# Loads for the norms asked for one norm earlier, and the wide tiles of x loaded once, in the sixth and ninth gate and up pass

## The chip, the cores and the metric

The kernel runs on one core of one Trainium2 chip. The metric is the device time of one execution, in microseconds (us).

## The reference, cut to what matters

`x` has 2048 rows of 512 numbers in fp32. Four layers follow each other, a Fourier mixing layer and a gated feed-forward layer, twice:

```python
x = x + A(layernorm(x))        # layer 0
x = x + B(layernorm(x))        # layer 1
x = x + A(layernorm(x))        # layer 2
x = x + B(layernorm(x))        # layer 3

def A(x):                      # real part of a DFT over the hidden and the row dimension
    a, b = x @ dft_hid_re.T, x @ dft_hid_im.T
    return dft_seq_re @ a - dft_seq_im @ b

def B(x):                      # w_gate, w_up: 512 x 1792, w_down: 1792 x 512
    return (gelu(x @ w_gate) * (x @ w_up)) @ w_down
```

## The kernel before, in words

**Products.** Every fp32 product is made of three matmuls (`mm3`, L208 to L210): both operands are split into a rounded part and a remainder (`split`: ScalarE copies the rounded part at L151, VectorE subtracts it at L153), and high by high, high by low and low by high are summed in PSUM. Blocks are multiplied by a scheme with seven products in place of eight (pieces named A11, A12, S1 to S4, A22), whose sums and differences are VectorE's (L184, L188, L191).

**Stages.** `mix(layer)` runs layers 0 and 2. `geglu(w, layer)` runs layers 1 and 3, each for two halves of the rows, w = 0 and w = 1 (1024 rows each). A half has 14 passes `up(n)` over the gate and up weights (7 products each), with the first products of the down projection between them (`beside(n)`: in an odd pass A11 of pair (n-1)//2, in an even one A12). Then comes the `late` list: the other down products, 36 of them when all seven pairs are done that way. `SEVEN` gives the pairs: seven in three halves (layer 1 w 0, layer 1 w 1, layer 3 w 0), where `pairs == NP`, and five in the last half (layer 3 w 1).

**The wide tiles.** The down projection's results are turned back by VectorE and added to `x` in a wide tile of 128 x 2048 fp32 (`turned_rows`), one for each 512 rows: part 0 in the buffer `xwide`, part 1 in the buffer `wide`. `load_turned(part)` (L1254) fills such a tile with four DMAs of 256 KB on SyncE's queue (L1258). `rows_done` (L1271) writes it out. In the kernel before, a half with seven pairs calls `load_turned(0)` twice: in pass 14 (`beside(13)`, L1230) and once more behind the passes (L1348). Nothing reads the first copy. `load_turned(1)` stands a third into the `late` list (L1385). The buffer `wide` is also that of the turned rows of the norms (L670), from which a DMA at L675 takes them to DRAM.

**The norms.** While w = 0 runs, the rows of w = 1 are normalized (`block_steps(layer, 1)`, `norm(i)`, eight of 128 rows), one every nine steps, a step being about a product. The first rows of w = 0 are normalized in the mix ahead of it. Each norm's rows come in four DMAs of 64 KB (`x_load_mixed`, L245). ScalarE then sums them (L564), sums the squares (L566), GpSimd makes the root (L567, L568), ScalarE scales (L590), VectorE turns (L672). L664 says which rows norm i asks for: norm 0 those of the norms 0, 1, 2, and norm i those of norm i + 2.

**Streams.** The weights of the down products come through a list of items on SyncE's queue (L327, tile `s<-wc`, one DMA each); `stream["last"]` is the newest of these DMAs. `too_far` (L331) holds such an item to two places ahead of its use in the passes and to six ahead in the `late` list (`NEAR`). The pieces of the gate and up weights are loaded at L1009 (`s<-wb`) two passes ahead; in layer 1 w 0 they are made from raw weights in place of that. In layer 1 w 1 the sums for the next layer's norms are made ahead (`terms_ahead`), with rows loaded one ahead at L236.

**Order.** `TileContext(nc, schedule_with_timeline_sim=True)` orders each engine's instructions by the times of a simulation at build time. So an instruction that nothing holds back may stand in its engine's queue far ahead of its place in the code; the queue itself runs in order. `tc.issue_after(ins)` puts what is made inside it behind `ins` on the same engine. SyncE issues most loads; GpSimd issues most stores.

**The other work of ScalarE in a pass.** It copies sums out of PSUM (L195, L202) and applies the gelu (L1019); PSUM banks come free by it, and TensorE goes on into them.

Of the kernel before, what the change touches and what calls it, by code (L numbers as in the profile page):

```python
# [21 lines left out]
NT = TB // P  # L22
# [15 lines left out]
FORE = {0: 4, 2: 4}  # L38
MADE = 5
LEAD = 3  # L40
NK = NS // 2
SEED_AT = 3
MIXED = 4
# [4 lines left out]
def fnet_geglu(ctx: ExitStack, tc: tile.TileContext, x_in, ws, wh, wgu, wdn, wdc, out):  # L48
# [32 lines left out]
    nc = tc.nc  # L81
# [235 lines left out]
    stream = {"loaded": 0, "split": 0, "used": 0, "more": 0}  # L317
# [129 lines left out]
    NP = NF // 2  # L447

    def down_order(layer, w):
# [6 lines left out]
        late = [("S1", k) for k in range(LEAD)]  # L456
        late += [p for k in range(n) for p in [("S2", k)] + [("S1", k + LEAD)] * (k + LEAD < n)]
        late.insert(LEAD + 2, up.pop())
# [195 lines left out]
    def block_steps(layer, w):  # L654

        zt, t, wide = {}, {}, {}
        turned = [dram.tile([P, NT * D], F32, name=f"t{layer}_{w}_{part}") for part in range(2)]

        def norm(i):

            def run():
                r0 = w * 2 * NT
                end = 2 * NT if w else i // NT * NT + NT
                for k in range(i if i == 0 or i + NT == end and not w else i + 2, min(i + 3, end)):  # L664
                    fresh["mixed", r0 + k] = x_load_mixed(layer, r0 + k)
                z = normed(layer, r0 + i, True)
                part, n = divmod(i, NT)
                if n == 0:
                    assert not sb.out("z")
                    wide[part] = tpool.tile([P, NT * D], F32, name="wide")  # L670
                to = wide[part].rearrange("p (b n t) -> p b n t", n=NT, t=32)
                nc.vector.transpose(to[:, :, n], z.rearrange("p (b t) -> p b t", t=32))  # L672
                sb.put(z)
                if n == NT - 1:
                    nc.gpsimd.dma_start(turned[part], wide.pop(part))  # L675
            return run

        def fetch(c):

            def run():  # L680
                for part in range(2):
                    v = zt[c, part] = sb.get()
                    for i in range(P // 32):
                        cols = turned[part][:, (c * 4 + i) * P:(c * 4 + i + 1) * P]
                        to = v[i * 32:(i + 1) * 32]
                        (nc.gpsimd if w == 0 else nc.sync).dma_start(
                            to.rearrange("p (j t) -> p j t", t=P), cols.rearrange("(j p) t -> p j t", p=32)
                        )
            return run

        def difference(a, b):
            v = sb.get()
            minus(v, a, b)
            return v

        def first(c):
            def run():
                v = t[f"B{1 + c // 2}1", c % 2] = zt.pop((c, 0))
                blocks[f"B{1 + c // 2}1", c % 2] = split_slot(v)
            return run  # L700

        def second(c):
            def run():
                v = zt.pop((c, 1))
                if c < 2:
                    t["B12", c] = v
                    t["T1", c] = difference(v, t["B11", c])
                    sb.put(t.pop(("B11", c)))
                else:
                    c0 = c - 2  # L710
                    t["T2", c0] = difference(v, t["T1", c0])
                    t["T3", c0] = difference(v, t["B12", c0])
                    sb.put(t.pop(("B12", c0)))
                    blocks["B22", c0] = split_slot(v)
                    sb.put(v)
            return run

        def fourth(c):
            def run():
                t["T4", c] = difference(t["B21", c], t["T2", c])  # L720
                sb.put(t.pop(("B21", c)))
            return run

        def divide(name, c):
            def run():
                blocks[name, c] = split_slot(t[name, c])
                sb.put(t.pop((name, c)))
            return run

        one = [norm(i) for i in range(2 * NT)]  # L730
        two = [fetch(c) for c in range(ND)] + [first(c) for c in range(ND)] + [second(c) for c in range(ND)]
        two += [fourth(c) for c in range(2)]
        two += [divide(name, c) for name in ("T2", "T3", "T1", "T4") for c in range(2)]
        return one, two
# [287 lines left out]
    def geglu(w, layer):  # L1022
# [69 lines left out]
        def up(n):  # L1092
            if n + 3 in making:
                making[n + 3][0]()
            if n + 2 in making:
                queue.extend(making[n + 2][1])
            if n > 2:
                for _ in range(DOWN_RUNS[3]):
                    if down_making:
                        down_making.pop(0)()  # L1100
            product(n, chain[n], "S2", "T2", False, True)
            u[n] = copied(chain[n])
            down = beside(n)
            next(down, None)
            side[n] = ps8.get()
            product(n, side[n], "S1", "T1", True, True)
            w4[n] = copied(side[n])
            next(down, None)
            first(n + 1)
            product(n, chain[n], "S3", "T3", False, True)  # L1110
            v = w4.pop(n)
            plus(v, v, chain[n])
            finished(n, 1, 1, v)
            sb.put(v)
            next(down, None)
            product(n, side[n], "S4", "B22", False, True)
            v = u.pop(n)
            plus(v, v, side[n])
            ps8.put(side.pop(n))
            finished(n, 0, 1, v)  # L1120
            sb.put(v)
            next(down, None)
            second(n + 1)
            if pairs == NP:
                for name, k in down_order(layer, w)[1][:max(0, n - EARLY_FROM) * EARLY_EACH]:
                    if k in h4:
                        prepared(name, k)
            product(n, chain[n], "A22", "T4", False, True)
            ps = chain.pop(n)
            if n % 2 == 0:  # L1130
                v = copied(ps)
                finished(n, 1, 0, v)
                sb.put(v)
            else:
                finished(n, 1, 0, ps)
            ps8.put(ps)
            for _ in down:
                pass
# [8 lines left out]
        pairs = SEVEN.get((layer, w), 0)  # L1147
# [73 lines left out]
        def beside(n):  # L1221

            if plain_down:
                return down_steps(n - LAG, 0) if n >= LAG else iter(())
            k = (n - 1) // 2
            if k >= pairs:
                return iter(())
            if n % 2:
                if k == pairs - 1:
                    load_turned(0)  # L1230
                bs["A11", k] = split_slot(h[2 * k, 0])
                return down_product("A11", k)
            if n:
                pair_combined(k)
                return down_product("A12", k)
            return iter(())
# [11 lines left out]
        def rows_moved(at, part, run):  # L1248

            for p in range(NT):  # L1250
                v = xturned[part][p * 32:(p + 1) * 32]
                run(v.rearrange("t (j e) -> t j e", e=P), turned_view(at, part)[p])

        def load_turned(part):  # L1254
            assert part or not sb.out("x")
            pool = tpool if part else upool
            xturned[part] = pool.tile([P, NT * D], F32, name="wide" if part else "xwide")
            rows_moved(layer, part, lambda v, outside: nc.sync.dma_start(v, outside))  # L1258

        def turned_rows(part, c, src):  # L1260

# [82 lines left out]
                slow.pop(0)()  # L1344
        if plain_down:
            load_rows(0)
        elif pairs == NP:
            load_turned(0)  # L1348
        if w == 0:
            queue.extend([None] * 4 + others[len(ahead_of_all):ND] + ([] if ahead_of_all else [None] * 4) + others[ND:])  # L1350
        elif before_mix:
# [19 lines left out]
        else:  # L1371
# [3 lines left out]
            for i, (name, k) in enumerate(late):  # L1375
                for more in late[i:i + EARLY + 1]:
                    prepared(*more)
                for _ in down_product(name, k):
                    pass
                if not before_mix or i % 3 == 0:  # L1380
                    step()
                if before_mix and i == len(late) // 2:
                    stream["more"] = MORE
                if i == len(late) // 3:
                    load_turned(1)  # L1385
                    if w == 0:
                        queue[:2 * len(ahead)] = [run for pair in zip(ahead, queue) for run in pair] + queue[len(ahead):2 * len(ahead)]
                while w == 0 and len(queue) > 2 * (len(late) - 1 - i):
                    step()
# [118 lines left out]
```

## Time and profile before

| | |
|---|---|
| median of 3 runs | 1611.77 us (1610.68 to 1614.64) |
| the profiled execution's own time | 1611.43 us |
| its span, first to last instruction | 1609.7 us |
| granted TensorE clock, mean | 0.998 of full speed |
| busy TensorE / VectorE / ScalarE / GpSimd | 99% / 70% / 55% / 17% |
| moved by DMA | 419.14 MB, mean 260 GB/s |

The span is shorter than the execution's own time by 1.7 us, which lie around the first and last instruction. A row of a group gives line, engine, operation, names as out<-in with buffer numbers left out, shapes and count. A row of the timeline gives the start and the length in us, the engine (SPq is SyncE's queue), the line, the count, and in brackets how long the engine was idle before it and what ended that. A row of the windows gives the busy time of each engine in a stretch, with the number of instructions, then the granted clock, the busy share of the DMA engines and the rate.

### The profile page before, as it was taken

To read this page: it belongs to the slowest core of one execution; us is meant where nothing else is said; L and a number is where in the kernel's file an instruction comes from. 1 tells how busy PE (TensorE), PEld (TensorE's weight loads), DVE (VectorE), ACT (ScalarE), POOL (GpSimd) and SP (SyncE) were. 2 spreads that over 40 slices of the span, in tenths; PEclk is the share of its full clock that TensorE was granted. 3 is DMA by queue.
4 is the path that set the end of the run, shared out by engine and by line. 5 is a ranking of instruction groups with operands and counts; after the bars stand their busy time and mean duration, and the time that the engine had idled before them with its cause. 6 is when DMAs were issued, how large, how long until landed. Compare 5 with 4: busy or idle time off the path is not lost.

```text
span 1609.7 us, 22615 instructions
## 1 busy us (share of the span) xinstructions
PE 1597.4 (99%) x7008; PEld 1316.5 (82%) x7008; DVE 1132.5 (70%) x1958; ACT 885.1 (55%) x1711; POOL 271.7 (17%) x469
## 2 busy tenths in 40 slices
PE   9999999999999999999999999999998999999998
PEld 6888888888888888888788888888887888888887
DVE  7997878787699783456879877777744457744574
ACT  8955466654767554546566636465444545433460
POOL 4112121242556101000040001101310000000001
PEclk9999999999999999999999999999999999999999
DMA  9878887996999899755896776878999576895445
GB/s 358 294 262 301 297 312 258 344 323 207 338 350 317 275 357 289 230 170 181 273 306 200 250 256 219 305 235 291 251 312 266 165 216 193 309 307 166 125 150 157
DMA packets 238872, 419.14 MB, mean 260 GB/s; under 512 B 28512, under 2 KB 66656, under 8 KB 237728
## 3 DMA queue, kind: packets, MB, share of 16 engines
q1 hardware_dynamic: 214512, 336.16, 65.3%
q0 software_dynamic: 24240, 81.55, 14.3%
q8 instruction: 55, 0.90, 0.2%
q14 instruction: 65, 0.53, 0.1%
HBM read 341.31 MB, written 76.28 MB: 259 GB/s over the span
## 4 chain that ended last, share of the span: by engine, by line
PE 94%; DMA 3%; DVE 1%; ACT 1%; issue 0%; SPq 0%; POOL 0%; DVEq 0%; ACTq 0%; POOLq 0%
PE p L208 31%; PE p L209 31%; PE p L210 31%; DMA s<-x 1%; DMA xwide<-x 1%; DMA s<-wc 1%; PE p L809 1%; DMA begun<-wide 0%; DVE s L153 0%; DMA s<-wb 0%; DVE s L184 0%; DMA s<-begun 0%; DVE s L188 0%; ACT s L151 0%; SPq L1271 0%
## 5 line engine op out<-in xcount | busy, mean ns | idle before, releaser
L209 PE MATMUL p<-s,s 128*128 128x512 f32 x2320 | 900.4, 390 | 0.0
L210 PE MATMUL p<-s,s 128*128 128x512 f32 x2320 | 893.7, 389 | 0.0
L208 PE MATMUL p<-s,s 128*128 128x512 f32 x2320 | 867.2, 390 | 5.9 <-ACT s L1019 4.4
L153 DVE TENSOR_TENSOR s<-s,s 128x512 fp32r<-128x512 f32 (+1 forms) x809 | 507.6, 661 | 126.7 <-ACT s L151 110.4
L151 ACT ACTIVATE s<-s 128x512 fp32r<-128x512 f32 (+1 forms) x809 | 454.5, 607 | 239.2 <-DVE s L184 65.9
L208 PEld LDWEIGHTS p<-s,s 128*128 128x128 f32 x2320 | 436.0, 188 | 98.7 <-ACT s L1019 4.9
L209 PEld LDWEIGHTS p<-s,s 128*128 128x128 f32 x2320 | 436.1, 188 | 91.2 <-DVE s L153 1.0
L210 PEld LDWEIGHTS p<-s,s 128*128 128x128 f32 x2320 | 436.2, 188 | 90.7
L188 DVE TENSOR_TENSOR s<-s,p 128x512 f32<-128x512 f32 x188 | 127.2, 683 | 166.8 <-PE p L210 136.9
L184 DVE TENSOR_TENSOR s<-s,s 128x512 f32<-128x512 f32 (+1 forms) x374 | 222.8, 612 | 5.6 <-PE p L209 3.6
L195 ACT ACTIVATE s<-p 128x512 f32<-128x512 f32 x232 | 134.6, 594 | 123.2 <-PE p L210 119.7
L1019 ACT ACTIVATE s<-s 128x512 f32<-128x512 f32 x84 | 52.8, 629 | 60.2 <-DVE s L188 50.5
L567 POOL TENSOR_SCALAR rstd<-rstd 128x1 f32<-128x1 f32 x40 | 20.5, 512 | 363.3 <-ACT s L566 347.4
L153 DVE TENSOR_TENSOR s<-xwide,s 128x512 fp32r<-128x512 f32 x71 | 47.7, 678 | 33.5 <-ACT s L151 33.2
L313 POOL DMA_DIRECT2D wb<-s x84 | 46.6, 569 | 87.8 <-ACT s L151 67.6
L1033 DVE TENSOR_TENSOR s<-s,p 128x512 f32<-128x512 f32 x56 | 38.3, 684 | 32.3 <-PE p L210 29.6
L151 ACT ACTIVATE s<-xwide 128x512 fp32r<-128x512 f32 x71 | 43.0, 621 | 15.5 <-DVE xwide L184 6.6
L1019 ACT ACTIVATE s<-p 128x512 f32<-128x512 f32 x28 | 16.7, 597 | 63.3 <-PE p L210 59.8
L590 ACT ACTIVATE s<-s,shift,rstd 128x512 f32<-128x512 f32 x56 | 44.9, 811 | 10.9 <-DMA s<-x 4.9
L202 ACT ACTIVATE p<-p 128x512 f32<-128x512 f32 x56 | 32.8, 586 | 30.6 <-PE p L210 30.4
L191 DVE TENSOR_TENSOR s<-s,s 128x512 f32<-128x512 f32 (+1 forms) x68 | 40.6, 605 | 8.6 <-DMA s<-ws 6.7
L564 ACT ACTIVATE s<-s 128x512 f32<-128x512 f32 x33 | 20.7, 626 | 46.4 <-DMA s<-x 27.9
(100 smaller groups left out, 613.4 us busy)
## 6 DMA issues: line engine op xcount, KB each, us to landing
s<-ws SPq DMA_DIRECT2D x384, 256.0 KB, 4.9
s<-wb SPq DMA_DIRECT2D x294, 256.0 KB, 5.0
s<-wc SPq DMA_DIRECT2D x182, 256.0 KB, 4.4
s<-wh SPq DMA_DIRECT2D x116, 256.0 KB, 5.1
wb<-s POOLq DMA_DIRECT2D x98, 256.0 KB, 5.4
s<-x SPq DMA_DIRECT2D x59, 256.0 KB, 5.3
xwide<-ws SPq DMA_DIRECT2D x50, 256.0 KB, 4.6
wc<-s POOLq DMA_DIRECT2D x49, 256.0 KB, 5.6
```

The costliest lines, as they stand in the source:

```text
L151: newest["ACT"] = nc.scalar.activation(hi, src, AF.Copy)
L153: newest["DVE"] = nc.vector.tensor_tensor(lo, src, f32(hi), op=ALU.subtract)
L184: nc.vector.tensor_tensor(out, a, b, op=ALU.subtract)
L188: bank_read["DVE"] = nc.vector.tensor_tensor(out, a, b, op=ALU.add)
L191: nc.vector.tensor_tensor(out, a, b, op=ALU.add)
L195: bank_read["ACT"] = nc.scalar.activation(v, src, AF.Copy)
L208: nc.tensor.matmul(ps, ah, bh, start=start, stop=False, skip_group_check=True)
L209: nc.tensor.matmul(ps, ah, bl, start=False, stop=False, skip_group_check=True)
L210: nc.tensor.matmul(ps, al, bh, start=False, stop=stop, skip_group_check=True)
L313: nc.gpsimd.dma_start(a, f32(t))
L590: nc.scalar.activation(z, x, AF.Identity, bias=shift, scale=rstd)
L1019: nc.scalar.activation(t, g, AF.Gelu_apprx_tanh)
```

## The change

Rows for the norms: norm 0 of a block asks for the rows of four norms, and norm i for those of norm i + 3. Part 0 of the wide tiles is loaded once, in pass n = 5 of each half with seven pairs; the second load, behind the passes, is gone. Part 1 is loaded in pass n = 8 where w is 1; where w is 0 it stays a third into the `late` list. All these loads, part 1 included, are ordered behind the newest DMA of the stream. The last half (five pairs) keeps its loads as they were.

```diff
+TURNED = 5,8
...
                 end = 2 * NT if w else i // NT * NT + NT
-                for k in range(i if i == 0 or i + NT == end and not w else i + 2, min(i + 3, end)):
+                for k in range(i if i == 0 or i + NT == end and not w else i + 3, min(i + 4, end)):
                     fresh["mixed", r0 + k] = x_load_mixed(layer, r0 + k)
...
             down = beside(n)
             next(down, None)
+            if pairs == NP and n in TURNED[:1 + w]:
+                load_turned(TURNED.index(n))
             side[n] = ps8.get()
...
             if n % 2:
-                if k == pairs - 1:
+                if k == pairs - 1 and pairs < NP:
                     load_turned(0)
...
             xturned[part] = pool.tile([P, NT * D], F32, name="wide" if part else "xwide")
-            rows_moved(layer, part, lambda v, outside: nc.sync.dma_start(v, outside))
+            with tc.issue_after(stream["last"].ins) if pairs == NP else ExitStack():
+                rows_moved(layer, part, lambda v, outside: nc.sync.dma_start(v, outside))
...
         if plain_down:
             load_rows(0)
-        elif pairs == NP:
-            load_turned(0)
...
                 if i == len(late) // 3:
-                    load_turned(1)
+                    if w == 0 or pairs < NP:
+                        load_turned(1)
```

## The prediction, made blind

> **What bounds the kernel now.** I read the page first, then the waits of TensorE, then windows round its longest wait, then the timeline there. The page and the waits:
>
> ```profile
> PE 1597.4 (99%) x7008; PEld 1316.5 (82%) x7008; DVE 1132.5 (70%) x1958; ACT 885.1 (55%) x1711; POOL 271.7 (17%) x469
> ```
>
> ```profile
> PE p L208 <- ACT s L1019: 4.4, 1, 4.4
> PE p L1418 <- POOL ident masks.py:199: 1.4, 1, 1.4
> PE p L208 <- DMA s<-wc: 1.1, 1, 1.1
> PE p L208 <- ACT s L195: 0.3, 1, 0.3
> ```
>
> TensorE is busy for 99% of the span. So a change that takes no matmul away can win only TensorE's waits and what follows them. The 1.4 us are the start. One wait of 4.4 us, for a gelu (L1019), is the only large one. Its surroundings, in windows:
>
> ```profile
> 1200.00:1216.00 16.00, 16.00 (x73) 13.23 (x72) 5.70 (x9) 8.74 (x20) 2.46 (x4) 1.00 1.09 308
> 1207.00:1222.00 15.00, 13.89 (x62) 11.16 (x60) 6.72 (x10) 6.29 (x17) 2.46 (x4) 1.00 0.99 240
> 1219.00:1235.00 16.00, 11.56 (x41) 9.08 (x40) 5.11 (x8) 8.37 (x18) 1.35 (x3) 0.79 1.00 292
> 1225.00:1230.00 5.00, 4.68 (x11) 3.75 (x12) 1.07 (x2) 4.50 (x10) 1.35 (x3) 0.50 1.03 362
> ```
>
> In 16 us TensorE issues 73 matmuls ahead of the wait, 0.219 us each, and 41 in the 16 us round it. The 32 that are missing are 7.0 us: 4.4 us idle, and about 2.6 us because the clock granted behind the wait is 0.50 (11 matmuls in 5 us, where 23 would go). So this place costs 7.0 us, 0.43% of the time. [...]
>
> Who made TensorE wait, from the timeline of SyncE, ScalarE and TensorE:
>
> ```profile
> 1206.83 2.58 SPq L1258 DMA_DIRECT2D xwide<-x  x4
> 1209.51 3.54 SPq L1009 DMA_DIRECT2D s<-wb  x3
> 1213.14 4.10 SPq L245 DMA_DIRECT2D s<-x  x4
> 1218.38 2.01 SPq L1258 DMA_DIRECT2D xwide<-x  x3
> ```
>
> ```profile
> 1222.79 0.63 ACT L564 ACTIVATE s<-s 128x512 f32<-128x512 f32 x1 [6.47 <-DMA s<-x]
> 1224.12 0.57 ACT L195 ACTIVATE s<-p 128x512 f32<-128x512 f32 x1
> 1224.69 0.58 ACT L1019 ACTIVATE s<-p 128x512 f32<-128x512 f32 x1
> 1225.32 0.80 PE L208 MATMUL p<-s,s 128*128 128x512 f32 x1 [4.44 <-ACT s L1019]
> ```
>
> This is the first pass of layer 3, w = 0. ScalarE's next instruction is the sum of norm 4's row (L564). It stands 6.47 us idle for that row, and the copy and gelu that empty TensorE's banks are queued behind it. The row was issued at 1213.14, behind 1 MB of the wide tile x at 1206.83 and three weight pieces. That wide load is the one that the code places in pass 14, and the repeat of 1218.38 is the one from behind the passes; nothing held either back. The landings in this case:
>
> ```profile
> L1258 SPq DMA_DIRECT2D xwide<-x x28: 303/443/3896, 408.5 to 1433.0; - x28
> L1258 SPq DMA_DIRECT2D wide<-x x16: 302/480/1963, 519.3 to 1422.0; - x16
> DMA to landing us min/median/max: 3.7/8.1/12.2
> ```
>
> ```profile
> DMA to landing us min/median/max: 1.7/3.1/8.3
> ```
>
> The upper three rows are the wide loads, the lower one the rows of L245: this row took the longest of all, 8.3 us against a median of 3.1.
>
> **The change part by part.**
>
> **The repeat goes.** 28 DMAs into xwide are 4 each for 2 + 2 + 2 + 1 loads; 12 go, 3.1 MB of 419 MB, and 12 x 0.443 = 5.3 us of SyncE's issue. None of it is on TensorE's path except in the place above: gain there counted below, elsewhere 0, hidden by a TensorE that waits nowhere else.
>
> **Part 0 moves behind the stream.** In pass n = 5 the stream's fifth piece is used; two places ahead makes its seventh the newest DMA. Counting `s<-wc` from each half's first, the seventh, for w = 1 the tenth in pass n = 8, and for part 1 with w = 0 (26th used, six ahead) the 32nd, are issued here:
>
> ```profile
> 444.32 0.34 SPq L327 DMA_DIRECT2D s<-wc  x1
> 637.27 0.32 SPq L327 DMA_DIRECT2D s<-wc  x1
> 1234.36 0.32 SPq L327 DMA_DIRECT2D s<-wc  x1
> 673.84 0.32 SPq L327 DMA_DIRECT2D s<-wc  x1
> 563.45 0.91 SPq L327 DMA_DIRECT2D s<-wc  x2
> 1359.89 1.33 SPq L327 DMA_DIRECT2D s<-wc  x3
> ```
>
> So in layer 3 the load cannot stand before about 1234, and 1 MB leaves the way of the row. At the 240 GB/s of the window 1207 to 1222, 1.05 MB are 4.4 us. With the row 4.4 us earlier, ScalarE's sum, copy and gelu come 4.4 us earlier, and of TensorE's 4.44 us nothing is left. That is just enough, without reserve.
>
> **Rows one norm earlier.** Norm 4's row is asked for with norm 1, not 2. How much earlier it is issued the trace doesn't show: at least 0, at most the 21 us between row 3's and row 4's issue:
>
> ```profile
> 1192.08 2.27 SPq L245 DMA_DIRECT2D s<-x  x4
> 1238.87 1.87 SPq L245 DMA_DIRECT2D s<-x  x4
> 1256.15 1.77 SPq L245 DMA_DIRECT2D s<-x  x4
> ```
>
> ```profile
> 633.55 0.63 ACT L564 ACTIVATE s<-s 128x512 f32<-128x512 f32 x1 [4.00 <-DMA s<-x]
> 1274.31 0.63 ACT L564 ACTIVATE s<-s 128x512 f32<-128x512 f32 x1 [0.78 <-PE p L210]
> 1284.96 0.63 ACT L564 ACTIVATE s<-s 128x512 f32<-128x512 f32 x1 [0.55 <-PE p L209]
> ```
>
> A slot is what limits it. I take some microseconds, the reserve that the step above lacks. The price is one more of 98 slots held for a norm; nothing waits for slots on TensorE, so 0.
>
> **What the moved loads meet.** Behind 1234.36 come rows 6 and 7 (1238.87, 1256.15), which are used at 1274.31 and 1284.96: 35 and 29 us later, against landings of at most 12.2. No wait. And a wait of ScalarE for a row need not reach TensorE: in layer 1, w = 1, it stood 4.00 us at 633.55, and TensorE has no wait there in the list above; at 1222.79 TensorE lost 2 us less than ScalarE. At 673.84 the part 1 load of w = 1 leaves the crowded start of that half. Part 1 with w = 0 moves from 519.3 to about 563 in layer 1, and to about 1360 in layer 3; it and the tile of w = 1 are needed at:
>
> ```profile
> 589.24 0.69 DVE L191 TENSOR_TENSOR wide<-wide,s 128x512 f32<-128x512 f32 x1
> 1399.76 0.68 DVE L191 TENSOR_TENSOR wide<-wide,s 128x512 f32<-128x512 f32 x1
> 799.74 0.65 DVE L191 TENSOR_TENSOR wide<-wide,s 128x512 f32<-128x512 f32 x1
> ```
>
> 563.5 and some 3 us of issue and 12.2 of landing make 579, 10 us ahead of need; the others have more. So 0, and if that cover went, a wait of VectorE at the end of the half. The waits of 1.1 and 0.3 us stay: no load of this change stands ahead of them.
>
> **Sum.** 1611.43 of the profiled execution - 7.0 = 1604.4. The median of the runs is 0.34 above that execution, so **1604.8**. The unknown: if only half of the 4.4 us come, 2.2 us of waiting are left, with the whole slow clock behind them or none, so the gain is 2.2 to 4.8 and the time 1607.0 to 1609.6; if the waits of 1.1 and 0.3 go as well, in a new order, 1603.4. The lowest of the three runs before is 1.1 below their median; half of that below 1603.4 is the low end, 1602.8.
>
> **The rivals.** About 0.3%, 4.8 us, is what a measurement of this kernel can tell from no change.
>
> **The wait moves.** All orders come from a simulation that places each instruction as early as it thinks data is there. So ScalarE's sums are again put just behind a row's expected landing, and a moved MB can delay another row:
>
> ```profile
> 1232.00:1247.00 15.00, 15.00 (x68) 12.43 (x67) 6.46 (x10) 5.18 (x9) 0.00 (x0) 1.00 0.87 255
> 560.00:576.00 16.00, 16.00 (x73) 13.24 (x72) 16.00 (x28) 13.30 (x25) 0.00 (x0) 1.00 0.95 310
> ```
>
> At 1232 to 1247 the DMA share is 0.87, so there is a queue to stand in. The same price, 7.0, is paid elsewhere, and the time is 1611.8; one smaller stop gives 1607 to 1611. Against it: the slack of 29 us and more above. The load not being held at all, should the seventh piece be drawn ahead of 1220, gives 1611.8 too. [...]
>
> **Slower: the late list runs dry.** In the late list of layer 1, w = 0, VectorE is busy 16.00 of 16 us from 560 to 576, and the DMA share is 0.95. There the change sets 1 MB among the stream's DMAs (563.45) that before went at 519. What the stream lands in, by the page:
>
> ```profile
> s<-wc SPq DMA_DIRECT2D x182, 256.0 KB, 4.4
> ```
>
> A piece of the late list is issued six places ahead of its use at the latest, 6 x 6 matmuls x 0.219 = 7.9 us, and lands 4.4 after issue: 3.5 us in hand. The MB costs 1.05 MB / 310 GB/s = 3.4 us. So it decides as soon as anything else holds these DMAs up by some tenths; then TensorE stops as at 1221, for 7.0, here and again at 1360 in layer 3: 1611.8 - 7.0 + 14.0 = 1618.8. Against it: 563.45 is drawn far ahead of the six places where slots are free, and TensorE has no wait there now.
>
> **How the numbers follow.** The forecast, wait gone: 0.50, 1602.8 to 1606.9. The wait moved, shortened or not touched: 0.34, 1607 to 1614. Late list dry, or another stop of that size in a new order: 0.16, 1617 to 1621. So faster 0.50, within 0.3% 0.34, slower 0.16. The range 1602.8 to 1615 leaves out the last case and little else.
>
> **What would show it.** Right: xwide loads x16, the layer 3 one behind 1234; no idle of ScalarE over 2 us before L564 near 1220; the wait for L1019 gone and the granted clock 1.00 there; rows of L245 landing under 6 us; wide<-x at about 563, 674, 1360. Wrong: a new wait of TensorE of over 3 us with a clock of 0.50 behind it, above all behind a wide load, or matmuls waiting for `s<-wc` at 565 to 600.

## The result and the profile after

| | before | after |
|---|---|---|
| median of the runs | 1612.0 us (1609.72 to 1614.64, 14 runs) | 1608.81 us (1606.79 to 1610.55, 14 runs) |
| the profiled execution | 1611.43 us | 1609.65 us |
| its span | 1609.7 us | 1607.9 us |

The ratio is 0.9979, with a 95% interval of 0.9971 to 0.9987: 3.2 us faster, 0.2%. The interval stays under 1, so there is a gain, but it lies within the 0.3% that was called no change. The forecast was 1604.8. In the changed kernel the lines shift by one to four: `mm3` is L209 to L211, the rows of the norms L246, the wide loads L1262, the stream L328, the pieces of the gate and up weights L1010.

The busy times and the waits of TensorE (engine, line, the tile waited for: us in all, times, longest) in the changed kernel:

```profile
PE 1595.9 (99%) x7008; PEld 1316.0 (82%) x7008; DVE 1134.1 (71%) x1958; ACT 884.5 (55%) x1711; POOL 270.7 (17%) x469
```

```profile
PE p L209 <- DVE s L154: 3.3, 1, 3.3
PE p L810 <- DMA s<-ws: 1.5, 1, 1.5
PE p L1421 <- POOL ident masks.py:199: 1.4, 1, 1.4
PE p L209 <- DMA s<-wc: 0.9, 1, 0.9
```

The 4.4 us for the gelu are gone. In their place stands one wait of 3.3 us, on a line of matmuls, put down to VectorE. Where each of them lies, the windows show (busy time and count of TensorE, weight load, VectorE, ScalarE, GpSimd, then the granted clock, the DMA share, GB/s); first the changed kernel, then the kernel before in the second place:

```profile
1219.00:1235.00 16.00, 16.00 (x73) 13.24 (x72) 5.69 (x9) 9.41 (x20) 1.35 (x3) 1.00 1.03 311
1356.00:1372.00 16.00, 12.72 (x48) 9.80 (x47) 12.49 (x21) 7.63 (x14) 0.00 (x0) 0.89 1.08 336
```

```profile
1356.00:1372.00 16.00, 16.00 (x72) 13.21 (x71) 16.00 (x28) 8.88 (x16) 0.00 (x0) 1.00 1.01 359
```

At 1219 there are 73 matmuls where there were 41: 32 x 0.219 = 7.0 us come back, as forecast. At 1356 there are 48 where there were 72: 24 x 0.22 = 5.3 us are lost. The difference, 1.7 us, is nearly the whole difference of the spans (1.8). Setting each of the 7008 matmuls beside the matmul of the same number in the kernel before says the same: 7.1 us won at 1220, 5.3 lost at 1360, 0.7 won in small steps between 400 and 770, about 1.1 lost in the first 20 us, 0.3 won at the end. The 1.1 us are the wait of 1.5 us for `s<-ws` in the list, at 7.4 us from the start; no other kernel's trace has more than 0.5 us there, so it belongs to this one execution and not to the change.

So the answer to "where did the gain go" is a place, 140 us behind the old one, in the late list of layer 3, w = 0. TensorE, SyncE's queue and VectorE there, in the changed kernel:

```profile
1358.48 0.61 PE L209 MATMUL p<-s,s 128*128 128x512 f32 x2
1362.38 0.47 PE L209 MATMUL p<-s,s 128*128 128x512 f32 x1 [3.28 <-DVE s L154]
```

```profile
1349.95 2.83 SPq L1262 DMA_DIRECT2D wide<-x  x4
1352.89 2.29 SPq L328 DMA_DIRECT2D s<-wc  x1
1355.23 0.43 SPq L1010 DMA_DIRECT2D s<-wb  x1
```

```profile
1357.42 1.88 DVE L154 TENSOR_TENSOR s<-s,s 128x512 fp32r<-128x512 f32 x3
1359.23 1.28 DVE L185 TENSOR_TENSOR s<-s,s 128x512 f32<-128x512 f32 x2
1360.43 1.88 DVE L154 TENSOR_TENSOR s<-s,s 128x512 fp32r<-128x512 f32 x3
```

The stop is the first product of the *next* half (w = 1): the build's order sets it among the late products of w = 0. Its two operands are a split row tile and a weight piece `s<-wb`. A piece comes in two DMAs, one for the rounded part and one for the remainder; the stopped matmul, high by high, needs the rounded part. Its DMA was issued at 1355.23, behind the four DMAs of the wide load (1 MB). The landing of that one DMA:

```profile
s<-wb SPq DMA_DIRECT2D x1, 256.0 KB, 7.0
```

1355.23 + 7.0 = 1362.2, just ahead of the matmul at 1362.38. VectorE's L154 also ends there (1360.43 + 1.88 = 1362.31), so the list of waits names it. Both fit by time, and this list alone doesn't tell them apart. The experiments decide.

In the kernel before, the two DMAs of the same piece were issued at 1358.46 and 1359.37, with no wide load ahead of them, and the product stood later in TensorE's order (about 1364):

```profile
1358.46 0.38 SPq L1009 DMA_DIRECT2D s<-wb  x1
1359.37 0.42 SPq L1009 DMA_DIRECT2D s<-wb  x1
```

How long the megabyte holds the queue can be read too. In the changed kernel its four DMAs land at 1356.7, 1358.1, 1359.6 and 1361.2, the stream's piece just ahead of them at 1355.3: 5.9 us for 1 MB, where weight pieces of the same 256 KB behind it land 0.7 us apart. All that the queue issued from 1344 to 1368 landed in the order of issue. The traffic from 1355 to 1356 in the changed kernel, and from 1350.1 to 1356.6 in the experiment below that puts that load later, so that nearly all of it is weights:

```profile
DMA packets 354, 0.18 MB, mean 177 GB/s; under 512 B 8, under 2 KB 354, under 8 KB 354
DMA packets 1354, 2.47 MB, mean 381 GB/s; under 512 B 149, under 2 KB 149, under 8 KB 1353
```

The wide load moves at about half the rate, in packets of some 0.5 KB (0.18 MB / 354) where the weights have nearly 2 KB. Whether the packets' size is the reason, no run here tests.

### The profile page after: what moved, and what is told of

It reads as the page before. It is cut to its first block, busy times and chain, and to the rows that moved or that the text cites. A ratio compares the mean times of both kernels' runs of the same rounds, so it can differ in the third digit from the quotient of the medians.

```text
span 1607.9 us, 22597 instructions
## 1 busy us (share of the span) xinstructions
PE 1595.9 (99%) x7008; PEld 1316.0 (82%) x7008; DVE 1134.1 (71%) x1958; ACT 884.5 (55%) x1711; POOL 270.7 (17%) x469
## 4 chain that ended last, share of the span: by engine, by line
PE 79%; issue 13%; DMA 4%; DVE 2%; POOL 1%; ACT 1%; SPq 0%; POOLq 0%; DVEq 0%; ACTq 0%
PE p L210 26%; PE p L209 26%; PE p L211 26%; DMA s<-t 1%; DVE s L154 1%; DMA s<-x 1%; DMA s<-begun 1%; PE p L810 1%; DMA wide<-x 1%; DMA xwide<-x 1%; DMA xwide<-t 0%; POOL rstd L568 0%; DMA s<-wc 0%; DMA begun<-xwide 0%; DVE s L189 0%
## 5 line engine op out<-in xcount | busy, mean ns | idle before, releaser
L211 PE MATMUL p<-s,s 128*128 128x512 f32 x2320 | 893.5, 389 | 0.0
L209 PE MATMUL p<-s,s 128*128 128x512 f32 x2320 | 868.5, 390 | 4.2 <-DVE s L154 3.3
L154 DVE TENSOR_TENSOR s<-s,s 128x512 fp32r<-128x512 f32 (+1 forms) x809 | 508.3, 662 | 122.6 <-ACT s L152 103.0
L209 PEld LDWEIGHTS p<-s,s 128*128 128x128 f32 x2320 | 435.7, 188 | 96.6 <-DVE s L154 3.7
L211 PEld LDWEIGHTS p<-s,s 128*128 128x128 f32 x2320 | 436.0, 188 | 90.6
L1020 ACT ACTIVATE s<-s 128x512 f32<-128x512 f32 x84 | 52.9, 629 | 63.1 <-DVE s L189 62.8
L568 POOL TENSOR_SCALAR rstd<-rstd 128x1 f32<-128x1 f32 x40 | 23.9, 598 | 365.7 <-ACT s L567 350.9
L154 DVE TENSOR_TENSOR s<-xwide,s 128x512 fp32r<-128x512 f32 x71 | 47.8, 680 | 34.1 <-ACT s L152 33.9
L980 POOL DMA_DIRECT2D wc<-s x42 | 30.5, 728 | 55.0 <-ACT s L152 37.9
```

Of the source, the lines that this page charges most:

```text
L154: newest["DVE"] = nc.vector.tensor_tensor(lo, src, f32(hi), op=ALU.subtract)
L209: nc.tensor.matmul(ps, ah, bh, start=start, stop=False, skip_group_check=True)
L211: nc.tensor.matmul(ps, al, bh, start=False, stop=stop, skip_group_check=True)
L1020: nc.scalar.activation(t, g, AF.Gelu_apprx_tanh)
```

## The experiments

Each time is the median of 5 to 12 runs, with the lowest and the highest; each ratio is to the kernel before, run in the same series, with a 95% interval.

The theory: in layer 3 the megabyte of part 1 with w = 0, held behind the 32nd piece of the stream, delays the first weight piece of the next half. The rival: VectorE is late there, as the list of waits says, or some other part of the change costs the 5.3 us.

**The late load free.** The load of part 1 with w = 0 isn't ordered any more, in both layers:

```diff
-            with tc.issue_after(stream["last"].ins) if pairs == NP else ExitStack():
+            with tc.issue_after(stream["last"].ins) if pairs == NP and (w or not part) else ExitStack():
```

> The changed kernel, but part 1 of the wide tile in the two halves w = 0 is not ordered behind the stream, so it is issued where it was before the change (after the norms have left that buffer, some 50 us ahead of the late list in layer 3). Theory A, the megabyte that now stands in the late list of layer 3 delays the first weight piece of the next half, for which TensorE already waits there: the wait of 3.3 us at 1359 and the slow clock behind it (5.3 us together by the count of matmuls) go, and the time is 1608.8 - 5.3 = 1603.5, 1603 to 1605. Rival B, VectorE's splits are late there, as the list of waits names them: the wait stays and the time is 1608 to 1610.

1604.15 us (1603.19 to 1605.11), ratio 0.9948 [0.9936, 0.9961]. The loads went to 517 in layer 1 and to 1290 in layer 3, and the stop at 1358 is gone. The waits of TensorE in this kernel:

```profile
PE p L1421 <- POOL ident masks.py:199: 1.4, 1, 1.4
PE p L209 <- DMA s<-wc: 0.8, 2, 0.6
PE p L210 <- DVE s L154: 0.5, 1, 0.5
```

The theory holds so far (1603 to 1605 were expected of it). But this kernel also changes VectorE's order.

**The late load behind that piece.** The sharper test: the load stays late, even later than in the changed kernel, but behind the first weight piece of the next half.

```diff
-            nc.sync.dma_start(f32(t), wblocks[n][:, at:at + 512])
+            piece = nc.sync.dma_start(f32(t), wblocks[n][:, at:at + 512])
+            if n == i == 0:
+                stream["piece"] = piece
...
-            with tc.issue_after(stream["last"].ins) if pairs == NP else ExitStack():
+            behind_it = stream["piece" if part and not w else "last"] if pairs == NP else None
+            with tc.issue_after(behind_it.ins) if pairs == NP else ExitStack():
...
+                if pairs == NP and w == 0 and i == len(late) // 2:
+                    load_turned(1)
                 if i == len(late) // 3:
-                    if w == 0 or pairs < NP:
+                    if pairs < NP:
                         load_turned(1)
```

> The changed kernel, with the part 1 load of w = 0 asked for half way into the late list and put behind the first weight piece of the next half (the one that the stopped matmul at 1359 needs) instead of behind the 32nd piece of the stream. Theory A: the stop is that piece waiting in the queue behind the megabyte. With the piece ahead of it the stop of 3.3 us and the slow clock behind it go, and the time is 1603 to 1605.5; nothing but the order of these DMAs differs. Rival B: whatever is issued behind the megabyte in this stretch stops TensorE: the stop moves to a later piece of s<-wb or s<-wc, 2 to 4 us at 1360 to 1375, and the time is 1606.5 to 1610.

1604.33 us (1602.9 to 1605.47), ratio 0.9943 [0.9924, 0.9962]. SyncE's queue and the window, in this kernel:

```profile
1350.47 0.32 SPq L1010 DMA_DIRECT2D s<-wb  x1
1350.88 0.39 SPq L328 DMA_DIRECT2D s<-wc  x1
1351.32 0.43 SPq L1010 DMA_DIRECT2D s<-wb  x1
...
1356.20 2.74 SPq L1265 DMA_DIRECT2D wide<-x  x4
```

```profile
1356.00:1372.00 16.00, 16.00 (x72) 13.22 (x71) 15.95 (x27) 12.12 (x22) 0.00 (x0) 1.00 1.10 308
```

The piece's two DMAs, at 1350.47 and 1351.32, landed in 4.4 and 4.9 us, not 7.0. (They also go out some 5 us sooner than in the changed kernel, so more differs than the order of these DMAs.) The megabyte comes later still, the DMA share is even higher (1.10), VectorE is as busy as ever (15.95 of 16), and TensorE issues its 72 matmuls at a clock of 1.00. So it is neither the megabyte as such nor VectorE, but that piece behind it. The rival that a later piece stops in its place is wrong.

**Half of it, and three quarters, free.** In layer 3 the first two (then three) of the four DMAs of that load are free, and the others stay ordered.

```diff
-            with tc.issue_after(stream["last"].ins) if pairs == NP else ExitStack():
-                rows_moved(layer, part, lambda v, outside: nc.sync.dma_start(v, outside))
+            moved = []
+
+            def run(v, outside):
+                free = layer == 3 and part and not w and len(moved) < 2
+                moved.append(v)
+                with tc.issue_after(stream["last"].ins) if pairs == NP and not free else ExitStack():
+                    nc.sync.dma_start(v, outside)
+
+            rows_moved(layer, part, run)
```

> The changed kernel, with the first two of the four DMAs of layer 3's part 1 load of w = 0 free of the order and the other two still behind the 32nd piece: half a megabyte ahead of the weight piece at 1360 instead of a whole one. Theory A, by bytes in the queue: the piece lands some 2 us sooner, TensorE's wait of 3.3 us falls to 0.5 to 1.7 us, the clock stays at 1.00 behind it, and the time is 1604 to 1606. Rival B: it isn't the bytes but that the piece is issued late, by SyncE's own place in the order: the wait stays at 2.5 to 3.5 us, and the time is 1607.5 to 1610.

1606.83 us (1605.13 to 1608.04), ratio 0.996 [0.9948, 0.9973]: between the two expectations. The wait, the issue and landing of the DMA that was waited for, and the window behind it, in this kernel (the build issues the remainder first here, at 1350.34):

```profile
PE p L209 <- DMA s<-wb: 2.6, 1, 2.6
```

```profile
1351.52 0.38 SPq L1010 DMA_DIRECT2D s<-wb  x1
```

```profile
s<-wb SPq DMA_DIRECT2D x1, 256.0 KB, 8.3
```

```profile
1358.00:1364.00 6.00, 4.08 (x11) 3.29 (x12) 3.77 (x7) 1.62 (x3) 0.00 (x0) 0.72 1.05 387
```

Here the list of waits names the piece itself. It lands at 1351.52 + 8.3 = 1359.8, 2.4 us sooner than in the changed kernel, which is what theory A expected of half the bytes. But the build drew the product earlier too, so TensorE stood before it at 1357 and not 1358.7, and 2.6 us of waiting are left. The clock falls behind them (0.72 over these 6 us). Both had a part right.

> As the run with half of layer 3's part 1 load of w = 0 free, but three of the four DMAs free and one, a quarter megabyte, behind the 32nd piece. Theory A, bytes in the queue: the weight piece of the next half lands some 1 to 2 us sooner again than with half a megabyte, TensorE's wait falls under 1.5 us with the granted clock at 1.00 behind it, and the time is 1603.3 to 1605.3. Rival B: the order written at build draws the stopped product earlier as the load shrinks, so that TensorE arrives sooner by as much as the piece does: the wait stays at 2 us or more, and the time is 1605.8 to 1607.5.

1604.35 us (1603.99 to 1605.69), ratio 0.9957 [0.9945, 0.997]. What is left of the wait in this kernel, put down to VectorE again:

```profile
PE p L209 <- DVE s L154: 0.7, 1, 0.7
```

The piece's DMA went out at 1350.85 and landed 6.5 us later, 2.5 us sooner than with half a megabyte; the product was drawn 0.6 us earlier. A quarter of a megabyte ahead of the piece costs 0.7 us and no slow clock (1.00 from 1358 to 1364): theory A. With 1, 1/2 and 1/4 MB ahead of the piece, TensorE waited 3.3, 2.6 and 0.7 us there. With the load free (in both layers, or in layer 3 alone) or behind the piece, its longest wait in the whole kernel but the start's was 0.6, 0.4 and 0.6 us.

**Late, but from the start of the late list.** The load is still ordered, but asked for when the late list begins.

```diff
+            if pairs == NP and w == 0:
+                load_turned(1)
...
-                    if w == 0 or pairs < NP:
+                    if pairs < NP:
                         load_turned(1)
```

> The changed kernel, but part 1 in the halves w = 0 is asked for at the beginning of the late list in place of a third into it, still ordered behind the stream; in the build it stands among the last fetches of the turned rows, about 15 DMAs ahead of its place in the changed kernel. Theory A: the first weight piece of the next half is not behind it any more; the stop at 1359 goes, 1603 to 1605, if the fetches that the megabyte now delays (they feed the blocks of the same first product) do not take its place; if they do, 1606 to 1611 with VectorE or ScalarE idle for these fetches. Rival B, VectorE late whatever the load: a stop of the same size, 1608 to 1610.

1605.9 us (1604.57 to 1607.96), ratio 0.9962 [0.9949, 0.9974]. Three of its DMAs go out at 1332 to 1334, the fourth at 1346, and TensorE waits little:

```profile
PE p L209 <- DMA s<-wb: 1.2, 1, 1.2
```

That is between the two times of theory A; rival B, a stop of the same size, is wrong. The 1.2 us are left although no wide load stands just ahead of the piece: its DMA went out at 1353.40 and landed 5.4 us later, and the product was drawn earlier again, so that TensorE stood before it from 1357.7 (1359.1 in the changed kernel). How much of this the fetches of the turned rows make is not shown.

The kernels that stop there also settle what the list of waits left open. The DMA lands at 1362.24, 1359.79, 1357.30 and 1358.78 (the whole load behind the stream, half of it, a quarter of it, and the load from the start of the late list), and the stopped matmul starts at 1362.38, 1359.92, 1357.43 and 1358.91: 0.13 to 0.14 us behind the landing each time, whether the list names VectorE or the DMA.

**The order lifted in layer 3 alone.** Is the load that moved in layer 1 (563) free?

```diff
-            with tc.issue_after(stream["last"].ins) if pairs == NP else ExitStack():
+            with tc.issue_after(stream["last"].ins) if pairs == NP and (w or not part or layer == 1) else ExitStack():
```

> The changed kernel, with the order of the part 1 load of w = 0 lifted in layer 3 alone; in layer 1 it stays behind the 32nd piece (563). Theory A: all of the loss lies at 1360 in layer 3, and the load that moved in layer 1 is free: the time is that of the run in which both layers were freed, 1603.2 to 1605.2, with no wait of TensorE over 1.5 us. Rival B: the load in layer 1 also costs something, in matmuls that are late by tenths without a single long wait: the time is 1605.5 to 1607.

1603.67 us (1602.31 to 1604.42), ratio 0.994 [0.9919, 0.996], the lowest median of all, though its interval doesn't part it from the kernels at 1604.15 and 1604.33. No wait but the start is over 0.4 us. So the move in layer 1 costs nothing that can be measured, and the loss lies at 1358 in layer 3. In layer 1 of the changed kernel a piece `s<-wb` also follows the megabyte, at 565.26, and lands 8.1 us later. But the list of the changed kernel has no wait for `s<-wb`, so this piece came in time.

**The rows alone, the loads alone.** The two halves of the change. The rows alone: the kernel before with

```diff
-                for k in range(i if i == 0 or i + NT == end and not w else i + 2, min(i + 3, end)):
+                for k in range(i if i == 0 or i + NT == end and not w else i + 3, min(i + 4, end)):
```

> The kernel before with the rows asked for one norm earlier and nothing else. In the build, the row of norm 4 in layer 3 then stands among the four DMAs of the wide load, not behind them and three weight pieces. Theory A, the megabyte ahead of the row made the wait of 4.4 us at 1221: at least a part of the megabyte is still ahead, so ScalarE still waits, and TensorE loses from 0 to 4.4 us there: 1606 to 1612, with the row landing over 6 us after its issue. Rival, it was the time of asking: the wait is gone and the time is 1605, with rows landing in about 3 us.

1606.59 us (1604.81 to 1610.43), ratio 0.997 [0.9959, 0.9981]. The loads alone: the changed kernel with that line as it was before.

> The changed kernel with the rows asked for as before, so the loads' part of the change alone. In the build, SyncE's order round 1210 is that of the kernel before without the wide load. Theory A: the row lands some 4.4 us earlier, the wait at 1221 is under 0.5 us, and the stop in the late list of layer 3 is there as in the changed kernel: 1608.8, 1608 to 1610. Rival, the rows' part is what took the wait away: ScalarE still waits over 5 us for the row, TensorE stops at both places, 1612 + 5.3 - 0 = 1615 to 1618.

1611.34 us (1609.17 to 1613.16), ratio 0.9996 [0.9987, 1.0005]. The waits and the window of the rows alone, then the waits and the windows of the loads alone:

```profile
PE p L208 <- ACT s L195: 1.3, 1, 1.3
```

```profile
1219.00:1235.00 16.00, 14.72 (x64) 11.47 (x64) 5.26 (x8) 9.18 (x19) 1.17 (x3) 1.00 1.00 267
```

```profile
PE p L209 <- DVE s L154: 4.1, 1, 4.1
```

```profile
1356.00:1372.00 16.00, 11.91 (x42) 9.30 (x41) 12.48 (x21) 7.37 (x13) 0.00 (x0) 0.79 1.09 324
1219.00:1235.00 16.00, 16.00 (x73) 13.24 (x72) 6.94 (x11) 10.14 (x20) 1.35 (x3) 1.00 0.98 299
```

The loads alone clear the wait at 1221 whole (73 matmuls), as theory A had it, and give nearly all of it back at 1360: 42 matmuls, 30 too few, 6.6 us. That is 1.3 us more than in the changed kernel, about half of the 2.5 us by which the time lies above the 1608.8 that was expected; the rest is open. The rows alone win most of it (64 matmuls, 23 more than before, 5.0 us), with the row's DMAs still landing after 6 to 8 us: theory A, and not the rival, which had no wait left. They lose 0.9 us at 1360 (68 matmuls from 1356 to 1372 in place of 72). So each half clears most of the old wait by itself, and only the loads carry the long new one.

**The repeat alone.** The kernel before without `elif pairs == NP: load_turned(0)`.

> The kernel before, with nothing changed but that the repeat of the part 0 load behind the passes is left out (12 DMAs, 3.1 MB of 419). Theory A: the row of norm 4 in layer 3 stands behind the first of the two loads, the one of pass 14, so the repeat costs nothing there: the wait for the gelu at 1221 stays at about 4.4 us with the granted clock at 0.50 behind it, and the time is that of the kernel before, 1610.5 to 1613. Rival B: the repeat (issued at 1218.38 in the kernel before, while the row was still landing) slows the row by sharing the DMA engines: without it the row lands at least 2 us sooner, the wait falls under 2.5 us, and the time is 1605 to 1608.

1611.53 us (1607.67 to 1613.17), ratio 0.9989 [0.9978, 1.0001]. ScalarE and TensorE in this kernel:

```profile
1222.53 0.63 ACT L564 ACTIVATE s<-s 128x512 f32<-128x512 f32 x1 [6.47 <-DMA s<-x]
```

```profile
PE p L208 <- ACT s L1019: 4.4, 1, 4.4
```

The same 6.47 and 4.4 us as before: the first copy is what delayed the row. 3.1 MB fewer are worth nothing that can be measured.

**Rows earlier and no repeat.** The two edits together; no load is ordered behind the stream.

> The kernel before, with rows one norm earlier and without the repeat of the part 0 load; no load is ordered behind the stream. Theory A: of what is left of the wait at 1221 in the run with the earlier rows alone (1.3 us), the repeat is no cause, since it is issued behind the row: the time is that of that run, 1605.5 to 1607.5, with 0.8 to 1.5 us of waiting near 1221. Rival B: with neither repeat nor late row nothing waits there: 1603.2 to 1605, and no wait of TensorE over 1 us but the start.

1607.41 us (1605.21 to 1608.5), ratio 0.9971 [0.9959, 0.9983]. Theory A had the time, but neither had the wait. TensorE, the window and SyncE's rows in this kernel:

```profile
PE p L208 <- ACT s L195: 2.6, 1, 2.6
```

```profile
1219.00:1235.00 16.00, 13.44 (x53) 10.54 (x52) 5.26 (x8) 7.69 (x17) 0.77 (x3) 0.89 0.93 296
```

```profile
1202.42 2.27 SPq L245 DMA_DIRECT2D s<-x  x2
...
1209.86 0.31 SPq L245 DMA_DIRECT2D s<-x  x1
...
1214.61 0.31 SPq L245 DMA_DIRECT2D s<-x  x1
```

The row's first DMA goes out 10.7 us earlier than before (1213.14), but the order draws its four DMAs apart, with the wide load's between them, and the last goes at 1214.61 and lands 7.9 us later, at 1222.5. ScalarE's sum starts at 1222.62, hardly sooner than before. What became shorter is what stands behind the sum: the copy follows it at 1223.25, 0.63 later, where before it came 1.33 after, and TensorE goes on as soon as that copy ends, where before it waited for the gelu behind the copy too. So asking earlier is a gain with little in hand, while taking the load away leaves no wait at all.

## Why the prediction was wrong, point by point

- **The place and its price: right.** 7.0 us were forecast for the place at 1221, and 7.0 by the windows (7.1 by the matmuls) came back. That the megabyte ahead of the row causes it is shown by the loads alone.
- **The repeat at nothing: right**, by the repeat alone: 0.9989, and its interval holds 1.
- **Part 0 behind the stream, "just enough": right in kind, too low in size.** With the loads alone the row goes out at 1210.91, 2.2 us earlier, and lands in 4.9 us, not 8.3. That makes 5.6 us, not 4.4: the megabyte ahead of this row delayed its issue (by 2.2 us) and its landing (by 3.4 us) both. The 4.4 came from the mean rate of a mixed stretch, 240 GB/s; the wide load itself moved at 177 (the changed kernel, 1355 to 1356), which gives 5.9 us for 1.05 MB. The 3.4 us of the rival "the late list runs dry", from 310 GB/s, were too low in the same way. The load in layer 3 went out at 1229.06, five microseconds ahead of the 1234 that I gave, because the stream's seventh piece itself was drawn earlier, and still behind the row. In the changed kernel ScalarE sums at 1219.08 without idle time ahead of it:

```profile
1219.08 0.62 ACT L565 ACTIVATE s<-s 128x512 f32<-128x512 f32 x1
```

- **Rows one norm earlier as a reserve: under-rated.** Alone it wins about 5 us. The sign that I named, rows landing under 6 us, did not come, and was not needed: the first row DMA at 1205.37 took 7.0 us, and nothing waited for it.
- **"What the moved loads meet ... So 0": the step that failed.** I set the late load of part 1, w = 0, against the first use of its own tile (VectorE at 1399.76) and, as a rival, against the stream `s<-wc`. I didn't ask which other DMA of SyncE's queue stands behind it and who waits for that one. At 1355 it was the first piece `s<-wb` of the next half, for a product that the build's order had drawn into the late list. The step was worth 5.3 us: 1604.4 + 5.3 = 1609.7, against 1609.65 of the profiled execution (that it fits to a tenth is luck: the other gains, 0.7 and 0.3, and the 1.1 lost at the start nearly cancel). The sign of being wrong that I named, a new wait of over 3 us behind a wide load with a clock of 0.50 behind it, is the one that came. With the step undone in layer 3 the time is 1603.67, and undone in both layers 1604.15, where 1604.8 was forecast.
- **The rivals.** "The wait moves" (0.34, 1607 to 1614) is what happened, in its form of one smaller stop, though in another place than the rows that I looked at. The piece behind the megabyte shows it: 7.0 us to land behind it, 4.4 and 4.9 ahead of it. "The late list runs dry" had one of its two places right, 1360 in layer 3, but by the wrong stream, and layer 1 pays nothing.
- **The moved loads** went out within some 8 us of where I said, but layer 3's earlier: part 0 at 1229.06, not 1234, and part 1 at 1349.95, not 1360:

```profile
452.42 3.64 SPq L1262 DMA_DIRECT2D xwide<-x  x4
632.88 2.02 SPq L1262 DMA_DIRECT2D xwide<-x  x4
1229.06 2.25 SPq L1262 DMA_DIRECT2D xwide<-x  x4
674.82 2.02 SPq L1262 DMA_DIRECT2D wide<-x  x4
563.14 2.08 SPq L1262 DMA_DIRECT2D wide<-x  x4
```

What stays open: why the runs of the changed kernel spread over 3.8 us. That the stop at 1358 differs in length from run to run would fit, but only one execution of it has a trace.

## What to carry to other kernels

When a large load is moved in a queue whose DMAs land in the order of issue, as SyncE's did here (1355.3 to 1362.2 us in the changed kernel), don't only ask whether its own tile comes in time: list the next DMAs behind it in its new place, and find the first instruction that waits for each, the next stage's too where an order made at build draws them together. Where a load has 40 us in hand, hold it behind the last small DMA that something waits for soon, or let it go early; of the places tried here, the one just ahead of that DMA was the worst (1608.81 us, against 1603.67 to 1606.83 with the load, or part of it, elsewhere). And where a list of waits names an engine that was busy all the time, look for a DMA that landed within some tenths of the same moment (here at 1362.24, where VectorE ended at 1362.31).

## What was not expected of the hardware

In these runs the clock also fell behind stops shorter than the 4.4 us of the kernel before, where it was 0.50 from 1225 to 1230. Behind the stop of 3.3 us in the changed kernel the granted clock was 0.50 too (the windows below). Behind the stop of 2.6 us with half of the load free it was 0.72 over 6 us, and with the rows earlier and no repeat it was 0.89 over the 16 us round such a stop. Behind 1.3 us (the rows alone) it was 1.00, and behind 1.5 us (the changed kernel, at 7.4) it was 1.00 up to 12. So of these stops the two of 1.3 and 1.5 us are not followed by the slow clock, and each one of 2.6 us or more is; whether a stop between them is, such as the 2.2 us that the prediction took for a wait half gone, and whether the same length always does the same, isn't shown.

The slow stretch is not as long as the stop, and doesn't begin with it. In the changed kernel TensorE went on at 1362.38, and the clock was still 1.00 for 0.7 us, then 0.50 until 1366.6:

```profile
1362.40:1363.10 0.70, 0.70 (x3) 0.32 (x3) 0.00 (x0) 0.00 (x0) 0.00 (x0) 1.00 1.03 380
1363.20:1366.50 3.30, 3.30 (x8) 2.54 (x9) 1.30 (x3) 0.61 (x2) 0.00 (x0) 0.50 1.05 386
1366.60:1368.00 1.40, 1.40 (x8) 1.15 (x7) 1.40 (x3) 1.02 (x2) 0.00 (x0) 1.00 1.06 389
```

The slow stretch lasts 3.4 us with the stops of 2.6, 2.6 and 3.3 us, and 6.8 us, twice that, with those of 4.1 and 4.4 us (a clock of 0.72 over 6 us, and of 0.89 and 0.79 over 16 us, make about as much at 0.50). In it the matmuls of the changed kernel stand 0.43 us apart in place of 0.226, some ten of them. They make about 1.9 us of the 5.3, and the delay of the stopped matmul the other 3.4.
